# First group's queries and keys through the SP and ACT queues, by halves of the heads

## The chip, the cores and the metric

The kernel runs on one core of one Trainium2 chip. The metric is the device time of one execution in microseconds (us). TensorE is called PE here, VectorE DVE, ScalarE ACT, GpSimd POOL and SyncE SP; each runs its own instructions in program order and waits for the others by semaphores.

## The reference

Sliding-window attention with sink keys, then a feed-forward layer with a quick GELU (cut to what is computed):

```python
# q, k, v: 4 batches x 8 heads x 768 rows x 64, fp32; n_sink = 4, window = 128
scores = scale * np.matmul(q, k.transpose(0, 1, 3, 2))
rel = pos[:, None] - pos[None, :]
keep = (pos[None, :] < n_sink) | ((rel >= 0) & (rel < window))
scores = np.where(keep, scores, -1000000000.0)
a = np.exp(scores - np.max(scores, axis=-1, keepdims=True))
a = a / (np.sum(a, axis=-1, keepdims=True) + 1e-09)
attn_out = np.matmul(a, v)
x = attn_out.transpose(0, 2, 1, 3).reshape(3072, 512)
h = x @ w_in                                  # 512 x 2048
out = (h * (1.0 / (1.0 + np.exp(-1.702 * h)))) @ w_out    # 2048 x 512
```

## The kernel before

The 3072 tokens are worked through in twelve groups `g` of 256 rows (three to a batch `b`), each of two blocks `i` of 128 rows. A group goes through three stages, and successive groups overlap: attention, `hidden` (w_in and GELU), `out_part` (w_out). The order of the instructions on every engine is the order in which the program writes them; nothing rearranges them. For the first groups that order is written out by hand (L495 to L657), then a loop runs.

Attention of a group. `load_qk(g)` issues four loads on POOL (L124), for q and k of the two blocks, 128 rows by 512 columns (eight heads of 64) each; a load from POOL also casts fp32 to fp16. They go to the tile `qkn`. `transposed_qk` turns `qkn` into `qkT` with the head columns on the partitions: for the early groups PE transposes 128x128 tiles into a PSUM bank and DVE or ACT copies the bank out (L161 to L165). The heads are handled in pairs: `hp` is 0 to 3, two heads to each, so one `hp` is one 128-column tile.

The four sink keys of a batch are copied from `qkT` into `kd` (`sink_keys`, L168). `sinks(g)` (L185) makes the sink scores of all four `hp` by eight matmuls, then DVE scales and masks them into `sn` (L197) and takes their row minimum into `m2` (L203). `scores(g, hp)` makes the window scores of one `hp` (L231, L233) in a bank `nat`; there are two such banks, so the scores of hp 2 must wait until the weights of hp 0 have been read out of theirs. `maxima(g, hp)` is three DVE instructions: a predicated copy (L247), a row maximum (L250) and the bias (L260), which uses `m2`. `weights(g, hp)` is four exponentials on ACT (L271), by that bias. `weights_transposed` brings them to `AT`; for the first group by PE and a copy on DVE or ACT. `upper` and `lower` cut out the triangles, on POOL (L347) or DVE (L329). `sink_terms` (L302, tile `ts`) needs the bias of all four `hp`; `sink_weights` (L311) and `sink_transposed` (L316) follow. `values` (L360 to L372) multiplies by `vs` (the sinks' values spread over 16 column groups, filled by `sink_values`, L177, and a cast of `sinkrows`, L462) and by `vn`, the group's values; `normal` divides by the row sums, and `x_transposed` gives `xT`. Then `hidden(0, 0)` begins (L420).

At the start, before any of that: SP loads `ident` and `sinkrows`, then eight small pieces of v (`vsr`); ACT loads three constants and then its table of the exponential (`preload_act_table`, L453); DVE clears tiles; POOL issues `load_qk(0)`, then `load_w_in(0)`, `load_qk(1)`, `load_v(0)` and the other three quarters of w_in. The part of the written-out order that matters here (`ahead(0, 0)` is `sinks(0)`, `scores(0, 0)`, `maxima(0, 0)`; `ahead(0, 1)` the last two for hp 1):

```python
    transposed_qk(0, (0,))
    sink_values(0)
    transposed_qk(0, (1,))
    sink_keys(0, nc.vector.tensor_copy)
    ahead(0, 0)
    ahead(0, 1)
    weights(0, 0)
    weights(0, 1)
```

Of the kernel before, what the change touches and what calls it, by code (L numbers as in the profile page):

```python
# [10 lines left out]
FP32 = mybir.dt.float32  # L11
# [6 lines left out]
P = 128  # L18
D = 64
# [16 lines left out]
def _own() -> np.ndarray:  # L36

    return np.triu(np.ones((P, P))).astype(np.float16)


def _sink_off(n_sink: int) -> np.ndarray:


    q, j = np.arange(P)[:, None], np.arange(n_sink)[None, :]
    m = np.zeros((P, 2, 8, n_sink), np.float32)
    m[:, 0] = BIG
    m[:, 1] = np.where(q >= j, 0.0, BIG)[:, None, :]
    return m.reshape(P, 16 * n_sink)
# [10 lines left out]
def kernel(  # L59
# [34 lines left out]
    vs = [big.tile([P, 16, D + 1], FP16, name=f"vs{b}") for b in range(B)]  # L94
    vsr = big.tile([64, B, D], FP32, name="vsr")
    pace = big.tile([1, 1], FP32, name="pace")

    def constant(eng, name, array, dt):
        d = nc.inline_tensor(array, name="c" + name)
        t = const.tile(list(array.shape), dt, name=name)  # L100
        eng.dma_start(t, d.ap())
        return t
# [4 lines left out]
    def av_bank(name, shape, dt=FP32):  # L107
        return psp.tile(list(shape), dt, tag="av", bufs=2, name=name)
# [17 lines left out]
    def load_qk(g: int):  # L126
        for part in range(4):
            load_part(g, part)

    def load_v(g: int):  # L130
        for part in (4, 5):
            load_part(g, part)

    def load_w_in(i: int):
        w = DF // 4
        nc.gpsimd.dma_start(
            w_in16[:, :, bass.ts(i, w)],
            moe_w_in[:, bass.ts(i, w)].rearrange("(c p) f -> p c f", p=P),
        )

    def load_w_out(i: int):
# [2 lines left out]
            moe_w_out[bass.ts(i, 512), :].rearrange("(c p) f -> p c f", p=P),  # L144
        )

    def transposed_qk(g: int, parts=range(2)):

        n = G[g]["qkn"]
        if 0 in parts:  # L150
            G[g]["qkT2"] = work.tile([P, 4 * HP, P], FP16, tag="qkT", bufs=4, name=f"qkT{g}")
        T = G[g]["qkT2"]
        if g >= EARLY:
            nc.sync.dma_start_transpose(T, n.rearrange("p a c -> p (a c)"))
        else:
            for part in parts:
                for a in (2 * part, 2 * part + 1):
                    first = g == 0 or (g == 1 and part == 0)
                    tp = (mm_bank if first else av_bank)(f"tqk{g}_{a}", (P, HP, P), FP16)
                    for c in range(HP):  # L160
                        nc.tensor.transpose(tp[:, c], n[:, a, bass.ts(c, P)], ident)  # L161
                    if (g == 1 and part == 0) or (g != 1 and a % 2 == 1):
                        nc.scalar.copy(T[:, bass.ts(a, HP)], tp)
                    else:
                        nc.vector.tensor_copy(out=T[:, bass.ts(a, HP)], in_=tp)  # L165
        G[g]["qkT"] = T.rearrange("p (e i c) s -> p e i c s", e=2, i=2)

    def sink_keys(b: int, copy):  # L168
        kT = G[b * NT]["qkT"]
        for h in range(2):  # L170
            copy(
                out=kd[b][bass.ts(h, D), :, bass.ts(h, n_sink)],
                in_=kT[bass.ts(h, D), 1, 0, :, 0:n_sink],
            )

    def sink_values(b: int):
        nc.vector.tensor_tensor(  # L177
            out=vs[b][0:64, :, 0:D],
            in0=vsr[:, b].unsqueeze(1).broadcast_to((64, 16, D)),
            in1=sink_rows[0:64].unsqueeze(2).broadcast_to((64, 16, D)),  # L180
            op=ALU.mult,
        )


    def sinks(g: int):  # L185

        b, t = divmod(g, NT)
        qkT = G[g]["qkT"]
        sk = av_bank(f"sk{g}", (P, 2, HP, 2 * n_sink))
        for i in range(2):  # L190
            for hp in range(HP):
                nc.tensor.matmul(sk[:, i, hp], qkT[:, 0, i, hp], kd[b][:, hp], start=True, stop=True)
        sn = work.tile([P, 16, n_sink], FP32, tag="sn", name=f"sn{g}")
        flat = sn.rearrange("p a j -> p (a j)")
        skf = sk.rearrange("p i a j -> p (i a j)")
        if t == 0:
            nc.vector.scalar_tensor_tensor(  # L197
                out=flat, in0=skf, scalar=-scale, in1=sink_off, op0=ALU.mult, op1=ALU.add
            )
        else:  # L200
            nc.vector.tensor_scalar(out=flat, in0=skf, scalar1=-scale, scalar2=None, op0=ALU.mult)
        m2 = work.tile([P, 2, HP, 2], FP32, tag="m2", name=f"m2{g}")
        nc.vector.tensor_reduce(out=m2.rearrange("p i c h -> p (i c h)"), in_=sn, axis=AX.X, op=ALU.min)  # L203
        G[g].update(sn=sn, m2=m2, bias=work.tile([P, 2, HP, 2], FP32, tag="bias", name=f"bias{g}"))

    def scores(g: int, hp: int):

# [35 lines left out]
    def maxima(g: int, hp: int):  # L243
        m1 = work.tile([P, 2, 2], FP32, tag="m1", name=f"m1{g}_{hp}")
        if ("whole", hp) in G[g]:
            nat = G[g]["whole", hp]
            nc.vector.copy_predicated(  # L247
                out=nat[:, :, :, P:], mask=kinds(take_prev, g % NT), data=nat[:, :, :, 0:P]
            )
            nc.vector.tensor_reduce(  # L250
                out=m1.rearrange("p h i -> p (h i)"), in_=nat.rearrange("p h i c -> p (h i) c")[:, :, P:],
                axis=AX.X, op=ALU.max,
            )
        else:
            for h in range(2):
                nc.vector.copy_predicated(
                    out=G[g]["nat", hp][h], mask=kinds(take_prev, g % NT)[:, h], data=G[g]["before", hp][h]
                )
            nc.vector.tensor_reduce(out=m1, in_=G[g]["mine", hp], axis=AX.X, op=ALU.max)
        nc.vector.scalar_tensor_tensor(  # L260
            out=G[g]["bias"][:, :, hp], in0=m1.rearrange("p h i -> p i h"), scalar=-scale,
            in1=G[g]["m2"][:, :, hp], op0=ALU.mult, op1=ALU.min,
        )

    def weights(g: int, hp: int):

        nat, bias = G[g]["nat", hp], G[g]["bias"]
        A = work.tile([P, 4, P], FP16, tag="A", bufs=4, name=f"A{g}_{hp}")
        for h in range(2):
            for i in range(2):  # L270
                nc.scalar.activation(  # L271
                    out=A[:, 2 * h + i], in_=nat[h][:, i], func=AF.Exp, bias=bias[:, i, hp, h : h + 1],
                    scale=scale,
                )
        G[g]["A", hp] = A
# [46 lines left out]
    def lower(g: int, hp: int, pool=False):  # L322

        AT, i0 = G[g]["AT", hp], int(g % NT == 0)
        lo = work.tile([P, 2, 2, P], FP16, tag="lo", bufs=4, name=f"lo{g}_{hp}")
        if pool:
            selected(lo, AT, i0, 1)
        else:
            nc.vector.tensor_tensor(  # L329
                out=lo[:, :, i0:], in0=AT[:, :, i0:], op=ALU.mult,  # L330
                in1=own.unsqueeze(1).unsqueeze(1).broadcast_to((P, 2, 2 - i0, P)),
            )
        G[g]["lo", hp] = lo
# [112 lines left out]


    ident = constant(nc.sync, "ident", np.eye(P, dtype=np.float16), FP16)
    load_qk(0)
    take_prev = constant(nc.scalar, "prev", _take_prev(), U16)  # L450
    sink_off = constant(nc.scalar, "sinkoff", _sink_off(n_sink), FP32)
    own = constant(nc.scalar, "own", _own(), FP16)
    nc.scalar.preload_act_table(AF.Exp)  # L453
    sink_rows = constant(nc.sync, "sinkrows", _sink_rows(), FP32)
# [3 lines left out]
    masked_l = const.tile([P, P], FP16, name="maskedl")  # L458
    masked_r = const.tile([P, P], FP16, name="maskedr")
    sinkA = [const.tile([P, P], FP16, name=f"sinkA{i}") for i in range(2)]  # L460
    nc.vector.memset(vs[0], 0.0)
    nc.vector.tensor_copy(out=vs[0][:, :, D : D + 1], in_=sink_rows.unsqueeze(2))  # L462
    nc.vector.memset(masked_l, -1000.0)
    nc.vector.memset(masked_r, 15624.0)
    for t_ in (*kd, *sinkA):
        nc.vector.memset(t_, 0.0)
    for row in vn:
        for t_ in row:
            nc.vector.memset(t_[:, :, :, D : D + 1], 1.0)
    zero_reg = nc.gpsimd.to_reg(0.0)  # L470
    load_w_in(0)
    load_qk(1)
    load_v(0)
    for i in (1, 2, 3):
        load_w_in(i)

    def sink_columns(b: int):
        nc.vector.memset(vs[b], 0.0)
# [2 lines left out]
    def ahead(n: int, hp: int):  # L481

        if n < NG:
            if hp == 0:
                sinks(n)
            scores(n, hp)
            maxima(n, hp)
# [4 lines left out]
                out_part(g, i, p)  # L492


    transposed_qk(0, (0,))  # L495
    sink_values(0)
    transposed_qk(0, (1,))
    sink_keys(0, nc.vector.tensor_copy)
    ahead(0, 0)
    ahead(0, 1)  # L500
    weights(0, 0)
    weights(0, 1)
    scores(0, 2)
# [1 line left out]
    maxima(0, 2)  # L505
    upper(0, 0)
    lower(0, 0, pool=True)
    weights(0, 2)
    scores(0, 3)
    maxima(0, 3)  # L510
    sink_terms(0)
    weights_transposed(0, 1, by_act)
    upper(0, 1)
    lower(0, 1, pool=True)
    sink_weights(0)
    weights(0, 3)
    sink_transposed(0)
# [242 lines left out]
```

## Time and profile before

| what | value |
|---|---|
| median of three runs | 256.85 us (254.86 to 257.67) |
| the profiled execution | 253.48 us |
| its span, first to last instruction | 251.8 us |
| PE busy | 220.5 us, 88% of the span |
| DVE, ACT, POOL busy | 60%, 61%, 40% |
| granted PE clock | 0.99 of full speed |
| moved by DMA | 32.86 MB, mean 131 GB/s |

The page of the profile gives the busy time of each engine, the same in 40 slices of the span, the DMA queues, the chain of work that ended last with each step's releaser, and the costliest groups of instructions. The trace behind it answers finer questions: the chain within a window, the instructions of a window in order of time with what ended the idle time before each, and the busy time of each engine by window. In the lists "ACTq" and "SPq" are the engines' sequencers, which issue DMAs; the time of such a row is that of the issue, not of the transfer.

### The profile page before, as it was taken

Reading aid. Unit: us, or ns where it says so; the run is one execution under the profiler, and the core shown is the slowest. Engines: PE = TensorE matmul, PEld = TensorE weight load, DVE = VectorE, ACT = ScalarE, POOL = GpSimd, SP = SyncE. Lnnn points to the kernel's source line nnn. Section 1 sums busy time; section 2 is a strip of 40 time slices with the busy share of each in tenths; the row PEclk is TensorE's granted clock in tenths of the full one; section 3 lists DMA queues with packets and bytes.
Section 4 is the critical chain, followed back from the end, with each engine's and each line's share of the span. In section 5 each row is a group of like instructions: output and inputs, shape, how many; then the busy total and the mean of one; then the engine's idle time right before and its main releaser. Section 6 shows DMA issues by size and latency. Waiting matters only on the chain.

```text
span 251.8 us, 5731 instructions
## 1 busy us (share of the span) xinstructions
PE 220.5 (88%) x2180; PEld 151.2 (60%) x2180; DVE 151.5 (60%) x397; ACT 153.9 (61%) x349; POOL 101.6 (40%) x154
## 2 busy tenths in 40 slices
PE   0437979797785999999999999999999999799993
PEld 0326756674354848738758569478486595494851
DVE  4686777386589647657768288477583783830101
ACT  2176575748457577676766875776777767751430
POOL 8848547423662825816624445356020220310000
PEclk9999999999998899999999999999999999999999
DMA  8999999989699999999999989999965623603102
GB/s 77 157 176 198 188 194 123 160 107 98 116 144 175 153 131 169 165 119 246 115 158 160 144 169 144 133 172 140 163 131 98 108 63 64 146 3 83 42 3 85
DMA packets 133612, 32.86 MB, mean 131 GB/s; under 512 B 126288, under 2 KB 130512, under 8 KB 133584
## 3 DMA queue, kind: packets, MB, share of 16 engines
q0 software_dynamic: 79104, 13.64, 73.7%
q1 hardware_dynamic: 54048, 18.73, 42.2%
q8 instruction: 17, 0.28, 0.5%
q10 hardware_dynamic: 432, 0.13, 0.2%
q14 instruction: 11, 0.09, 0.1%
HBM read 27.50 MB, written 6.29 MB: 134 GB/s over the span
## 4 chain that ended last, share of the span: by engine, by line
PE 51%; DVE 17%; ACT 16%; DMA 10%; issue 4%; POOL 0%; ACTq 0%; DVEq 0%; POOLq 0%; SPq 0%
PE hT L420 27%; PE o L435 12%; ACT A L271 7%; DVE m L250 5%; DVE nat L247 5%; DMA AT<-A 5%; ACT L423 4%; DMA xT<-xn 3%; PE av L372 2%; ACT L271 2%; ACT gT L423 2%; DMA qkn<-in_q_dram 2%; PE av L360 2%; PE av L368 2%; PE tqk L161 1%
## 5 line engine op out<-in xcount | busy, mean ns | idle before, releaser
L420 PE MATMUL hT<-xT,w_in 128*128 128x256 f16 x768 | 95.6, 275 | 5.4 <-ACT gT L423 2.4
L435 PE MATMUL o<-w_out,gT 128*128 128x512 f16 x384 | 89.6, 379 | 0.0
L420 PEld LDWEIGHTS <-w_in 128*128 128x128 f16 x768 | 72.8, 99 | 18.6 <-issue 3.5
L423 ACT ACTIVATE gT<-hT 128x512 f16<-128x512 f32 x96 | 56.5, 597 | 44.4 <-PE hT L420 44.2
L347 POOL TENSOR_SCALAR_AFFINE_SELECT up<-AT 128x512 f16<-128x512 f16 (+1 forms) x48 | 28.0, 588 | 103.6 <-DMA AT<-A 76.6
L271 ACT ACTIVATE A<-nat,bias 128x128 f16<-128x128 f32 x192 | 53.4, 383 | 24.4 <-DVE bias L260 19.2
L435 PEld LDWEIGHTS <-gT 128*128 128x128 f16 x384 | 34.9, 98 | 37.8
L247 DVE COPY_PREDICATED nat<-prev,nat 128x512 f32<-128x512 uint16 x40 | 27.7, 692 | 24.3 <-PE nat L233 11.1
L250 DVE TENSOR_REDUCE m<-nat 128x4 f32<-128x512 f32 x40 | 27.6, 691 | 1.4
L329 DVE TENSOR_TENSOR lo<-AT,own 128x512 f16<-128x512 f16 (+1 forms) x44 | 19.1, 448 | 5.8 <-DMA AT<-A 5.6
L124 POOL DMA_DIRECT2D qkn<-in_k_dram x24 | 21.3, 896 | 2.8 <-DMA w_out<-in_moe_w_out_dram 2.8
L124 POOL DMA_DIRECT2D qkn<-in_q_dram x24 | 21.6, 905 | 1.3 <-POOLq L741 0.8
L124 POOL DMA_DIRECT2D vn<-in_v_dram x24 | 21.2, 891 | 1.0 <-issue 0.8
L390 DVE TENSOR_TENSOR xn<-av,rcp 128x256 f16<-128x256 f32 x48 | 20.4, 424 | 1.7
L443 DVE COPY osb<-o 128x512 f32<-128x512 f32 x10 | 6.9, 691 | 23.2 <-PE o L435 23.2
L368 PE MATMUL av<-vn,up 128*128 128x65 f16 x160 | 18.6, 195 | 1.1 <-POOL up L347 1.1
L372 PE MATMUL av<-vn,lo 128*128 128x65 f16 x160 | 18.3, 196 | 0.7 <-POOL lo L347 0.6
L360 PE MATMUL av<-vs,AsT 128*128 128x130 f16 x80 | 16.6, 224 | 0.4 <-DVE xn L390 0.3
L389 DVE RECIPROCAL rcp<-av 128x4 f32<-128x4 f32 x48 | 8.5, 178 | 13.8 <-PE av L372 13.5
L368 PEld LDWEIGHTS <-up 128*128 128x128 f16 x160 | 14.9, 100 | 2.4 <-POOL up L347 1.3
L233 PE MATMUL nat<-qkT 64*128 64x128 f16 x272 | 16.0, 224 | 0.0
L233 PEld LDWEIGHTS <-qkT 64*128 64x128 f16 x352 | 11.4, 97 | 7.1 <-issue 6.9
(59 smaller groups left out, 184.6 us busy)
## 6 DMA issues: line engine op xcount, KB each, us to landing
out_dram<-osb SPq DMA_DIRECT2D x24, 256.0 KB
qkn<-in_q_dram POOLq DMA_DIRECT2D x24, 128.0 KB, 5.2
qkn<-in_k_dram POOLq DMA_DIRECT2D x24, 128.0 KB, 4.8
vn<-in_v_dram POOLq DMA_DIRECT2D x24, 128.0 KB, 6.4
w_in<-in_moe_w_in_dram POOLq DMA_DIRECT2D x4, 512.0 KB, 9.8
w_out<-in_moe_w_out_dram POOLq DMA_DIRECT2D x4, 512.0 KB, 10.1
AT<-A SPq DMA_TRANSPOSE x40
qkT<-qkn SPq DMA_TRANSPOSE x9
```

The costliest lines, as they stand in the source:

```text
L124: nc.gpsimd.dma_start(dst, (q, k, v)[e][b, :, rows].rearrange("h s d -> s h d"))
L233: nc.tensor.matmul(to[h][:, i], qkT[r, 0, i, hp], keys[r], start=True, stop=True)
L247: nc.vector.copy_predicated(out=nat[:, :, :, P:], mask=kinds(take_prev, g % NT), data=nat[:, :, :, 0:P])
L250: nc.vector.tensor_reduce(out=m1.rearrange("p h i -> p (h i)"), in_=nat.rearrange("p h i c -> p (h i) c")[:, :, P:], axis=AX.X, op=ALU.max,)
L271: nc.scalar.activation(out=A[:, 2 * h + i], in_=nat[h][:, i], func=AF.Exp, bias=bias[:, i, hp, h : h + 1], scale=scale,)
L347: nc.gpsimd.affine_select(out=out, in_=in_, pattern=[[0, rows], [sign, P]], compare_op=ALU.is_gt if sign < 0 else ALU.is_ge, fill=zero_reg ...
L360: nc.tensor.matmul(av[:, i].rearrange("p h d -> p (h d)"), AsT, vs[b][:, c : c + 2].rearrange("p h d -> p (h d)"), start=True, stop=False,)
L368: nc.tensor.matmul(av[:, i, h], up[:, h, i], vn[b][J // 2][:, J % 2, head], start=False, stop=False)
L372: nc.tensor.matmul(av[:, i, h], own_w[:, h, i], vn[b][t][:, i, head], start=(I == 0), stop=(I == 0 or h == 1))
L420: nc.tensor.matmul(hT[:, f], w_in16[:, c, bass.ts(F, P)], xT[:, :, c], start=(c == 0), stop=(c == 3))
L423: nc.scalar.activation(out=G[g]["gT"][:, 2 * F2 : 2 * F2 + 2].rearrange("p f s -> p (f s)"), in_=hT.rearrange("p f i s -> p (f i s)"), fun ...
L435: nc.tensor.matmul(o, gT[:, F, bass.ts(i, P)], w_out16[:, F], start=(F == 0), stop=(F == NF - 1))
```

## The change

The first group's q and k no longer come through POOL. Four new fp32 tiles `first[e][u]` (e: q or k; u: first or second half of the heads) are loaded without a cast, q from SP and k from ACT, two loads each (one a block); the first halves are issued before `prev` and `sinkoff`, the second halves after them and before `own` and the table load. DVE rounds the q halves to fp16, ACT the k halves (`first_rounded`). `first_transposed(u)` transposes half of the heads of q and k into one PSUM bank and copies it out in two copies. `sink_keys` and `sinks` take a range of `hp`, so that sink scores, `sn` and `m2` of the first group are made for hp 0 and 1 first, then for hp 2 and 3; other groups call them as before.

Around it the order changes: the memsets of the ones columns of `vn` move from DVE to POOL; `load_v(0)` becomes POOL's first load; w_in 2 and 3 are issued later, behind the triangles of hp 0 and of hp 1; the memset of `vs[0]` moves behind the other memsets, and its cast and `sink_values(0)` move from the start to behind `maxima(0, 3)`, ahead of `sink_terms(0)`.

```diff
+    first = [[big.tile([P, 2, 4 * D], FP32, name=f"first{e}_{u}") for u in range(2)] for e in range(2)]
...
+    def load_first(eng, e: int, u: int):
+
+        for i in range(2):
+            eng.dma_start(
+                first[e][u][:, i].rearrange("s (h d) -> s h d", h=4),
+                (q, k)[e][0, 4 * u : 4 * u + 4, bass.ts(i, P)].rearrange("h s d -> s h d"),
+            )
+
+    def first_rounded(e: int, u: int, copy):
+        copy(G[0]["qkn"][:, 2 * e : 2 * e + 2, bass.ts(u, 4 * D)], first[e][u])
+
+    def first_transposed(u: int, copies):
+        n = G[0]["qkn"]
+        T = G[0]["qkT2"].rearrange("p (e i c) s -> p e i c s", e=2, i=2)
+        tp = mm_bank(f"tqk0_{u}", (P, 2, 2, 2, P), FP16)
+        for e in range(2):
+            for i in range(2):
+                for c in range(2):
+                    nc.tensor.transpose(tp[:, e, i, c], n[:, 2 * e + i, bass.ts(2 * u + c, P)], ident)
+        for e in range(2):
+            copies[e](T[:, e, :, 2 * u : 2 * u + 2], tp[:, e])
...
-    def sinks(g: int):
+    def sinks(g: int, pairs=slice(0, HP)):
...
-            for hp in range(HP):
+            for hp in range(pairs.start, pairs.stop):
                 nc.tensor.matmul(sk[:, i, hp], qkT[:, 0, i, hp], kd[b][:, hp], start=True, stop=True)
...
     ident = constant(nc.sync, "ident", np.eye(P, dtype=np.float16), FP16)
-    load_qk(0)
+    load_first(nc.sync, 0, 0)
+    load_first(nc.scalar, 1, 0)
     take_prev = constant(nc.scalar, "prev", _take_prev(), U16)
     sink_off = constant(nc.scalar, "sinkoff", _sink_off(n_sink), FP32)
+    load_first(nc.sync, 0, 1)
+    load_first(nc.scalar, 1, 1)
     own = constant(nc.scalar, "own", _own(), FP16)
     nc.scalar.preload_act_table(AF.Exp)
...
-    nc.vector.memset(vs[0], 0.0)
-    nc.vector.tensor_copy(out=vs[0][:, :, D : D + 1], in_=sink_rows.unsqueeze(2))
+    for row in vn:
+        for t_ in row:
+            nc.gpsimd.memset(t_[:, :, :, D : D + 1], 1.0)
+    zero_reg = nc.gpsimd.to_reg(0.0)
     nc.vector.memset(masked_l, -1000.0)
     nc.vector.memset(masked_r, 15624.0)
     for t_ in (*kd, *sinkA):
         nc.vector.memset(t_, 0.0)
-    for row in vn:
-        for t_ in row:
-            nc.vector.memset(t_[:, :, :, D : D + 1], 1.0)
-    zero_reg = nc.gpsimd.to_reg(0.0)
+    nc.vector.memset(vs[0], 0.0)
+    load_v(0)
     load_w_in(0)
     load_qk(1)
-    load_v(0)
-    for i in (1, 2, 3):
-        load_w_in(i)
+    load_w_in(1)
...
-    transposed_qk(0, (0,))
-    sink_values(0)
-    transposed_qk(0, (1,))
-    sink_keys(0, nc.vector.tensor_copy)
-    ahead(0, 0)
-    ahead(0, 1)
+    first_rounded(0, 0, by_dve)
+    first_rounded(1, 0, by_act)
+    first_transposed(0, (by_dve, by_act))
+    first_rounded(0, 1, by_dve)
+    first_rounded(1, 1, by_act)
+    scores(0, 0)
+    scores(0, 1)
+    sink_keys(0, nc.vector.tensor_copy, slice(0, 2))
+    sinks(0, slice(0, 2))
+    maxima(0, 0)
+    first_transposed(1, (by_act, by_act))
+    maxima(0, 1)
+    sink_keys(0, nc.vector.tensor_copy, slice(2, HP))
+    sinks(0, slice(2, HP))
     weights(0, 0)
     weights(0, 1)
     scores(0, 2)
...
     maxima(0, 2)
     upper(0, 0)
     lower(0, 0, pool=True)
+    load_w_in(2)
     weights(0, 2)
     scores(0, 3)
     maxima(0, 3)
+    nc.vector.tensor_copy(out=vs[0][:, :, D : D + 1], in_=sink_rows.unsqueeze(2))
+    sink_values(0)
     sink_terms(0)
     weights_transposed(0, 1, by_act)
     upper(0, 1)
     lower(0, 1, pool=True)
+    load_w_in(3)
     sink_weights(0)
```

More of the change, by code (lines that the diff above doesn't have):

```diff
@@ L166, in transposed_qk, with sink_keys @@
         G[g]["qkT"] = T.rearrange("p (e i c) s -> p e i c s", e=2, i=2)
-    def sink_keys(b: int, copy):
+    def sink_keys(b: int, copy, pairs=slice(0, HP)):
         kT = G[b * NT]["qkT"]
@@ L171, in sink_keys @@
             copy(
-                out=kd[b][bass.ts(h, D), :, bass.ts(h, n_sink)],
-                in_=kT[bass.ts(h, D), 1, 0, :, 0:n_sink],
+                out=kd[b][bass.ts(h, D), pairs, bass.ts(h, n_sink)],
+                in_=kT[bass.ts(h, D), 1, 0, pairs, 0:n_sink],
             )
@@ L182, in sink_values @@
         )
-    def sinks(g: int):
+    def sinks(g: int, pairs=slice(0, HP)):
         b, t = divmod(g, NT)
         qkT = G[g]["qkT"]
-        sk = av_bank(f"sk{g}", (P, 2, HP, 2 * n_sink))
+        if pairs.start == 0:
+            G[g].update(
+                sn=work.tile([P, 16, n_sink], FP32, tag="sn", name=f"sn{g}"),
+                m2=work.tile([P, 2, HP, 2], FP32, tag="m2", name=f"m2{g}"),
+                bias=work.tile([P, 2, HP, 2], FP32, tag="bias", name=f"bias{g}"),
+            )
+        sk = av_bank(f"sk{g}_{pairs.start}", (P, 2, HP, 2 * n_sink))
@@ L190, in sinks @@
         for i in range(2):
-            for hp in range(HP):
+            for hp in range(pairs.start, pairs.stop):
                 nc.tensor.matmul(sk[:, i, hp], qkT[:, 0, i, hp], kd[b][:, hp], start=True, stop=True)
-        sn = work.tile([P, 16, n_sink], FP32, tag="sn", name=f"sn{g}")
-        flat = sn.rearrange("p a j -> p (a j)")
-        skf = sk.rearrange("p i a j -> p (i a j)")
+        if pairs == slice(0, HP):
+            sn4, m2f = G[g]["sn"], G[g]["m2"].rearrange("p i c h -> p (i c h)")
+            sn = sn4.rearrange("p a j -> p (a j)")
+            skp, off = sk.rearrange("p i a j -> p (i a j)"), sink_off
+        else:
+            sn4 = G[g]["sn"].rearrange("p (i c h) j -> p i (c h) j", i=2, h=2)[
+                :, :, 2 * pairs.start : 2 * pairs.stop
+            ]
+            sn = G[g]["sn"].rearrange("p (i a) j -> p i (a j)", i=2)[
+                :, :, 2 * n_sink * pairs.start : 2 * n_sink * pairs.stop
+            ]
+            m2f = G[g]["m2"].rearrange("p i c h -> p i (c h)")[:, :, 2 * pairs.start : 2 * pairs.stop]
+            skp = sk.rearrange("p i a j -> p i (a j)")[:, :, 2 * n_sink * pairs.start : 2 * n_sink * pairs.stop]
+            off = sink_off.rearrange("p (i a) -> p i a", i=2)[
+                :, :, 2 * n_sink * pairs.start : 2 * n_sink * pairs.stop
+            ]
@@ L196, in sinks @@
         if t == 0:
             nc.vector.scalar_tensor_tensor(
-                out=flat, in0=skf, scalar=-scale, in1=sink_off, op0=ALU.mult, op1=ALU.add
+                out=sn, in0=skp, scalar=-scale, in1=off, op0=ALU.mult, op1=ALU.add
             )
         else:
-            nc.vector.tensor_scalar(out=flat, in0=skf, scalar1=-scale, scalar2=None, op0=ALU.mult)
-        m2 = work.tile([P, 2, HP, 2], FP32, tag="m2", name=f"m2{g}")
-        nc.vector.tensor_reduce(out=m2.rearrange("p i c h -> p (i c h)"), in_=sn, axis=AX.X, op=ALU.min)
@@ L204, in sinks @@
-        G[g].update(sn=sn, m2=m2, bias=work.tile([P, 2, HP, 2], FP32, tag="bias", name=f"bias{g}"))
+            nc.vector.tensor_scalar(out=sn, in0=skp, scalar1=-scale, scalar2=None, op0=ALU.mult)
+        nc.vector.tensor_reduce(out=m2f, in_=sn4, axis=AX.X, op=ALU.min)
     def scores(g: int, hp: int):
@@ L492, in o @@
                 out_part(g, i, p)
-    transposed_qk(0, (0,))
-    sink_values(0)
-    transposed_qk(0, (1,))
-    sink_keys(0, nc.vector.tensor_copy)
-    ahead(0, 0)
-    ahead(0, 1)
+    G[0]["qkn"] = work.tile([P, 4, DM], FP16, tag="qkn", bufs=3, name="qkn0")
+    G[0]["qkT2"] = work.tile([P, 4 * HP, P], FP16, tag="qkT", bufs=4, name="qkT0")
+    G[0]["qkT"] = G[0]["qkT2"].rearrange("p (e i c) s -> p e i c s", e=2, i=2)
+    first_rounded(0, 0, by_dve)
[12 more added lines that the diff above has]
+    sinks(0, slice(2, HP))
     weights(0, 0)
```

## The prediction

> **What bounds the kernel now.** The page's first two blocks come first: TensorE is busy 88% of the span, and its row of slices is thin only at the start and the very end. So I read the chain of waits for the first 30 us, then the timeline of the same stretch. The chain (start, length, what):
>
> ```profile
> 1.31 1.00 POOL qkn L124
> 2.32 4.97 DMA qkn<-in_q_dram
> 7.34 0.62 PE tqk L161 x4
> ...
> 8.62 0.60 PE tqk L161 x4
> 9.24 0.44 DVE qkT L165
> ...
> 10.32 0.36 PE sk L192 x8
> ...
> 11.26 0.71 DVE nat L247
> 11.99 0.70 DVE m L250
> ...
> 18.18 0.23 DVE ts L302
> ...
> 18.43 0.27 ACT sinkA L311
> ...
> 24.53 1.03 PE hT L420 x8
> ```
>
> Three parts: to 9.7 the chain waits for q and k; from 11.26 to 18.18 VectorE runs four maxima one behind the other; then the sink weights, the last transposes and values lead to the first hidden matmul at 24.53. From there TensorE is fed: in the table of windows it is busy 8.5 to 8.7 of every 10 us from 20 to 60, and no hT matmul of the first group waits for w_in. I therefore take it that the end moves by what 24.53 moves.
>
> The timeline shows what lies beside the chain:
>
> ```profile
> 1.69 0.45 ACTq L101 DMA_DIRECT2D own<-cown  x1
> 2.18 1.28 ACT L453 ACT_TABLE_LOAD   x1 [2.18 <-issue]
> 3.36 0.20 DVE L462 CAST vs<-sinkrows 128x16 f16<-128x16 f32 x1 [1.34 <-DMA sinkrows<-csinkrows]
> 6.43 1.22 DVE L177 TENSOR_TENSOR vs<-vsr,sinkrows 64x1024 f16<-64x1024 f32 x1 [0.20 <-DMA vsr<-in_v_dram]
> 9.70 0.57 DVE L171 COPY kd<-qkT 64x16 f16<-64x16 f16 x2
> 14.89 0.69 DVE L247 COPY_PREDICATED nat<-prev,nat 128x512 f32<-128x512 uint16 x1 [0.48 <-PE nat L233]
> ```
>
> The table load stands behind ACT's constants. The vs product, 1.22, runs in VectorE's idle time. Between the maxima VectorE idles only once to speak of (0.48).
>
> **The loads.** Four POOL loads (0.90 to 1.01 each to issue) leave the head; their data was in at 5.2, 7.3, 8.0 and 8.6 or a little later, by when TensorE could use it. In their place come eight loads of 128 KB (128 rows, four heads, 256 B pieces), four each on SP and ACT. No row of the trace issues such a load. Nearest are the constants, 0.35 to 0.46 (one piece a row), and the vsr loads, 0.67 to 0.93 (strided pieces). I take 0.5 each, since the load covers 128 rows as the constants do, and keep 0.35 and 0.93. Landing: sinkrows was issued at 1.23 and used at 3.36, so 2.1 us of latency; the DMA rows of the first 4 us reach 269 GB/s, so the first four loads (0.5 MB) need about 2 us more at 250. The first halves are in near 4.3, against 7.3 and 8.6.
>
> A rule speaks against this. The Trainium skill, "DMA: Bandwidth & Descriptors", section "Issuing engines are not separate DMA queues", says that DMAs from any engine share the same 16 DMA engines, and that several issuers save only issue time. By that alone the data would come little earlier, and the time would be that of the third rival below. I set a row above it: in the DMA view of the first 10 us, in slices of 0.25, the DMA engines stand at 0 until 1.75 and mostly at 40 to 50% until 3.5; what fills them then is POOL's loads of q and k, which the change takes away. In that stretch issue time is the limit.
>
> **ACT's queue is the new head.** Its loads stand before the table load, and rounding k stands behind that. From 0.81: two loads 1.0, prev 0.37, sinkoff 0.46, two loads 1.0, own 0.45, table 1.28 give 5.4. In the trace the later vsr loads wait for the constants' completion counts (hardware loads take turns on eight counts); ACT's third and fourth load are then about the ninth and eleventh and wait for the first ones' landing: 0.6 more, so 6.0. Rounding k costs 0.59 (ACT's 128x512 copy), so 6.65; four transposes of k 0.62, 7.3; ACT's copy to qkT 0.59, 7.95. q is done beside that (its DVE rounding, 0.42 to 0.69 by the copies of f16 and f32, ends near 5). Then TensorE: two hp of scores at 0.4, so the half sinks start at 8.75 (kd's copies, 0.5, lie beside), 0.25 for them, sn 0.23 and m2 0.22 with 0.15 between: the first copy-predicate at 9.65 instead of 11.26. Lead 1.6. With 0.35 a load it is 2.0; with 0.93 the queue alone is 1.7 longer, of which the 0.6 wait is absorbed: lead 0.5.
>
> **VectorE gives it back.** Before, 11.26 to 18.18 is 6.92: four maxima at a pitch of 1.54 (11.26 to 12.80), that is 6.16, and 0.76 of small waits (0.48 for the scores of hp 2, the rest at hp 3 and ts). After, the same row holds: two maxima 3.08; kd's second half, two copies, 0.55; the way to TensorE and back for the second half sinks 0.34; second sn and m2 0.50 (two half-width instructions cost nearly what the whole ones did: 0.23 and 0.22 for 64 elements are mostly fixed); two maxima 3.1; the cast of sink columns 0.2; the vs product 1.26; hand-over 0.1. Sum 9.1. The scores of hp 2 and 3 are then no longer waited for: the weights of hp 0 (ACT, from 11.3, 1.15) free their bank at 12.5, before the second half sinks. So ts starts at 9.65 + 9.1 = 18.75 instead of 18.18: **0.6 later**. Behind ts stand the sink weights on ACT, behind them the weights of hp 3 (1.13), the last transposes, values, xT and the first hidden matmul. All of them wait, so 24.53 becomes 25.1. The vs product is 1.26 of this: its cover, the wait for q and k, is what the change leaves.
>
> **Costed at nothing.** Twelve memsets go from DVE (0.07 each, idle time) to POOL ahead of its first load: POOL's memsets start 0.03 apart, its slowest small copy takes 0.20, so 0.4 to 2.4. v's two loads still start by 4 instead of 9.13, and need at most 10.5 to land; values begin at 19.86. w_in 2 and 3 are issued near 16 and 18 instead of 13.1 and 14.1; at the worst landing of 11.9 they are in by 28 and 30, for first use near 30.5 and 32.5. That is enough, and POOL's stream is four loads shorter, so I charge 0, at worst 0.5. SP's vsr loads move behind four loads and are in by 12, used at 17.5. POOL's selects move with the weights.
>
> One more rule speaks against the roundings: the Trainium skill, "SBUF — State Buffer", section "SBUF: two separate sides", says that an fp32 SBUF copy on VectorE can lock GpSimd out of writing load descriptors. The trace has only a related case, the vs product beside POOL's loads at 5.66 to 7.48, which kept their 0.91. By the rule v's or w_in's issue would slip by the two roundings, up to 1.4; they have several us to spare, so the sum is the same.
>
> **Rivals.**
> 1. *Faster, downstream.* POOL's stream of loads is four loads shorter and starts w_in and v sooner, so it drains 2 to 3 us earlier near 44. Then the key transposes of group 3 and the loads of group 4 end sooner, and the weight transposes at 61.3 and 64.0 (2.43 and 3.16 on the chain) meet less traffic. If half of that falls away, 2.8 is gained: 0.6 - 2.8 = -2.2, 254.6; a third gives -1.3. Against: those loads are paced by POOL's place in the chain, so they come along with it.
> 2. *Slower, ACT's head.* A 512-piece load costs more than any row here shows. Each 0.1 us per load puts 0.4 on ACT's queue ahead of the table load. It decides from 1.15 us a load on: four times 0.65 is 2.6, less the 0.6 wait, gives 2.0, plus 0.6 is 2.6. At 1.3 us: +3.2, 260.0.
> 3. *It does not do what it says.* Eight loads share the DMA engines with prev, sinkoff and v; the first halves land no earlier than before (7.3). Then k is rounded at 7.9, transposed at 8.55, in qkT at 9.2, 1.25 later than forecast: +1.85, 258.7.
>
> **How the numbers follow.** The profiled execution took 253.48 with a span of 251.8 (1.7 around it); the median of the runs is 256.85, 3.4 above it. The sum, 253.48 + 0.6 = 254.1, carried to the median gives 257.45. The forecast case (leads of 2.0 to 0.5, so +0.2 to +1.7: 257.0 to 258.6) gets 0.52, the rivals 0.18, 0.18 and 0.12. Runs of one kernel spread by 2.8, so a median of three can be 1 to 1.5 off, and 1% (2.6 us) is about the least that tells a change here. Low end: a third of the waits of rival 1 with such noise, 255; high end: rival 2 at 1.3 us, 260. Above 1% slower: most of rival 2 (0.13), some of rival 3 (0.04) and the noise of the forecast (0.04), 0.21. Above 1% faster: half of rival 1 (0.09) and 0.02. The rest, 0.68, is within 1%.
>
> **What would show it.** Right: ACT's table load ends near 6, the first copy-predicate stands near 9.7, ts behind the vs product near 18.8, the first hT matmul near 25.1. Rival 2: ACT's loads over 1.1 us each. Rival 3: VectorE's first rounding not before 6.5. Rival 1: hT late as forecast, but the AT transposes of the 61 to 67 us stage shorter. I am wrong if ts starts before 18, that is if VectorE's second half of kd, sn, m2 and the vs product hide somewhere.

## The result and the profile after

The change makes the kernel slower. Twenty runs each have a median of 254.32 us before and 257.89 after; the ratio is 1.0135 (95% interval 1.0113 to 1.0157), 3.4 us. The profiled execution of the changed kernel took 259.53 (span 257.8), the third longest of its twenty; so its rows are read for order and cause and the sizes come from the ratios, which count only executions within 1.5% of the fastest of their kernel (17 of 20 here, 5 of 10 in e5_hold_own, 5 of 6 in g1_hw_all, all or all but one in the other new kernels, one of 453.28 us in e4_pool_halves being left out).

The chain of waits of the changed kernel at the start (start, length, what):

```profile
1.21 3.44 DMA first<-in_q_dram
4.67 9.56 DMA first<-in_k_dram
...
14.32 0.63 ACT qkn L337
14.99 0.62 PE tqk L166 x4
15.63 1.07 ACT qkT L337 x2
16.70 1.05 ACT A L311 x4
...
21.78 1.09 DVE vs L200
22.87 0.35 DVE ts L342
...
29.26 1.03 PE hT L460 x8
```

One load holds the chain from 4.67 to 14.23: the last of ACT's, the second block of k's second half of the heads. The first hidden matmul starts at 29.26 instead of 24.53. The timeline of ACT shows how it hangs together ("ACTq" rows are the issues of loads):

```profile
0.81 1.00 ACTq L151 DMA_DIRECT2D first<-in_k_dram  x2
...
3.29 1.77 ACTq L151 DMA_DIRECT2D first<-in_k_dram  x2
6.33 0.35 ACTq L102 DMA_DIRECT2D own<-cown  x1
6.71 1.28 ACT L496 ACT_TABLE_LOAD   x1 [6.71 <-DMA first<-in_q_dram]
8.01 0.62 ACT L337 CAST qkn<-first 128x512 f16<-128x512 f32 x1
9.78 0.58 ACT L337 COPY qkT<-tqk 128x512 f16<-128x512 f16 x1 [1.16 <-DVE qkT L334]
14.32 0.62 ACT L337 CAST qkn<-first 128x512 f16<-128x512 f32 x1 [3.95 <-DMA first<-in_k_dram]
```

Two things are to be seen. The table load, and with it the first rounding of k, waits until 6.71, because the issue of `own` in front of it waited until 6.33 for the completion count of an earlier load of q. And the second rounding of k finds ACT idle for 3.95: its data is not there. By the completion counts in the trace the eight loads, issued at 0.81 to 4.67, landed at 3.3 and 5.4 (k) and 4.7 and 6.3 (q) for the first half, at 7.9 and 9.1 (q) and 10.5 and 14.2 (k) for the second. POOL's loads of v and w_in, issued from 1.62 on, run beside them: the DMA packets of POOL's queue begin at 4.2.

The order on ACT adds a smaller loss behind that. The bias of hp 0 is ready at 13.5, but ACT's program has the late rounding and the two copies ahead of the exponentials of hp 0, so these start at 16.70 and the bank that the scores of hp 2 need comes free only after the first four of them, at 17.8. The prediction had that bank free at 12.5; here VectorE waits another 0.69 for those scores, ahead of its third predicated copy at 18.51.

### The profile page after: what moved, and what is told of

Read it like the earlier page. It is cut to its first block, busy times and chain, and to the rows that moved or that the text cites. A ratio compares the mean times of both kernels' runs of the same rounds, so it can differ in the third digit from the quotient of the medians.

```text
span 257.8 us, 5742 instructions
## 1 busy us (share of the span) xinstructions
PE 220.8 (86%) x2180; PEld 150.8 (59%) x2180; DVE 151.9 (59%) x390; ACT 155.4 (60%) x352; POOL 99.7 (39%) x162
## 4 chain that ended last, share of the span: by engine, by line
PE 54%; DVE 14%; DMA 14%; ACT 14%; issue 3%; ACTq 0%; SPq 0%; POOL 0%; DVEq 0%; POOLq 0%
PE hT L460 29%; PE o L475 13%; DMA xT<-xn 6%; ACT A L311 5%; DVE m L290 4%; DVE nat L287 4%; DMA first<-in_k_dram 4%; ACT L463 3%; DMA AT<-A 2%; PE av L412 2%; ACT gT L463 2%; PE av L400 2%; PE av L408 2%; PE nat L273 1%; DMA first<-in_q_dram 1%
## 5 line engine op out<-in xcount | busy, mean ns | idle before, releaser
L387 POOL TENSOR_SCALAR_AFFINE_SELECT up<-AT 128x512 f16<-128x512 f16 (+1 forms) x48 | 29.0, 609 | 111.9 <-DMA AT<-A 85.2
L369 DVE TENSOR_TENSOR lo<-AT,own 128x512 f16<-128x512 f16 (+1 forms) x44 | 17.3, 407 | 6.0 <-DMA AT<-A 5.9
L125 POOL DMA_DIRECT2D qkn<-in_k_dram x22 | 19.5, 895 | 2.6 <-DMA w_out<-in_moe_w_out_dram 2.3
L125 POOL DMA_DIRECT2D qkn<-in_q_dram x22 | 19.6, 899 | 0.8 <-issue 0.7
L400 PE MATMUL av<-vs,AsT 128*128 128x130 f16 x80 | 16.5, 223 | 0.7 <-DVE xn L430 0.7
L429 DVE RECIPROCAL rcp<-av 128x4 f32<-128x4 f32 x48 | 8.5, 178 | 12.9 <-PE av L412 12.5
```

Of the source, the lines that this page charges most:

```text
L125: nc.gpsimd.dma_start(dst, (q, k, v)[e][b, :, rows].rearrange("h s d -> s h d"))
L387: nc.gpsimd.affine_select(out=out, in_=in_, pattern=[[0, rows], [sign, P]], compare_op=ALU.is_gt if sign < 0 else ALU.is_ge, fill=zero_reg ...
L400: nc.tensor.matmul(av[:, i].rearrange("p h d -> p (h d)"), AsT, vs[b][:, c : c + 2].rearrange("p h d -> p (h d)"), start=True, stop=False,)
```

## The experiments

Three theories were set against each other. A: the loads on SP and ACT share the DMA engines with POOL's long stream and come off badly. B: they are issued too late, behind waits for completion counts. C: the excess lies in VectorE's new order, the vs product above all.

**POOL held.** One small copy on POOL, which reads the last k load, is put ahead of its first load:

```diff
+    nc.gpsimd.tensor_copy(out=pace, in_=first[1][1][0:1, 1, 0:1])
     load_v(0)
```

> POOL waits with all its loads (v, w_in, group 1) until the second half of k has landed; nothing else changes. Theory A (the loads on SP and ACT share the DMA engines with POOL's stream and get too little of them): the second half of k, rounded at 14.3 us in the changed kernel, is rounded near 8 to 9, the first hT matmul falls from 29.3 to about 25.5, and the time falls by 2 to 3.5 us below the changed kernel (ratio to before 1.000 to 1.006). Theory B (the second half of k is late because ACT issues it late, at 3.3 and 4.7 us, behind the waits for completion counts): it still lands after 11 us and the ratio stays above 1.01. Theory C (the excess lies in VectorE's order, the vs product ahead of ts): no change in the ratio, 1.013.

Ratio 1.0062 (1.0034 to 1.0091): more than half of the loss is gone. POOL's packets now begin at 10.0. ACT's timeline in this kernel:

```profile
3.31 1.45 ACTq L151 DMA_DIRECT2D first<-in_k_dram  x2
5.70 0.34 ACTq L102 DMA_DIRECT2D own<-cown  x1
6.08 1.28 ACT L496 ACT_TABLE_LOAD   x1 [6.08 <-DMA first<-in_q_dram]
7.37 0.62 ACT L337 CAST qkn<-first 128x512 f16<-128x512 f32 x1
9.14 0.58 ACT L337 COPY qkT<-tqk 128x512 f16<-128x512 f16 x1 [1.16 <-DVE qkT L334]
9.63 0.62 ACT L337 CAST qkn<-first 128x512 f16<-128x512 f32 x1
```

ACT issues its second pair of loads at nearly the same times as before (3.31 and 4.36 against 3.29 and 4.67), yet the second rounding no longer waits for data: the two loads landed at 7.4 and 8.0 instead of 10.5 and 14.2. That is theory A; B would have left them late. The ratio lies just above A's 1.000 to 1.006, below B's 1.01. The first hidden matmul starts at 26.75, a little later than A expected, since the first predicated copy still comes at 11.28: `own` and the table load have hardly moved.

**All eight loads ahead of the constants.**

```diff
     load_first(nc.sync, 0, 0)
     load_first(nc.scalar, 1, 0)
+    load_first(nc.sync, 0, 1)
+    load_first(nc.scalar, 1, 1)
     take_prev = constant(nc.scalar, "prev", _take_prev(), U16)
     sink_off = constant(nc.scalar, "sinkoff", _sink_off(n_sink), FP32)
-    load_first(nc.sync, 0, 1)
-    load_first(nc.scalar, 1, 1)
```

> All eight loads of the first group are issued ahead of prev and sinkoff; nothing else changes. Theory A: the last k load is issued near 3 us instead of 4.7 but still meets POOL's stream from 4 us on, so it lands between 9 and 12 us instead of 14.2, and the ratio to before is 1.005 to 1.012. Theory B: all halves are in by 7.5 us, the first hT matmul near 25.5, ratio 1.000 to 1.005. Theory C: ratio 1.013.

Ratio 1.0114 (1.0054 to 1.0175) from four executions. It lies within A's range and above all of B's, but the interval also holds C's 1.013, so the rows have to decide. k's second half, now issued at 1.83 and 2.39, landed at 6.3 and 8.4; but the last load of q, which SP issued at 3.34 (it waits for a count), landed at 11.3, and now VectorE waits for that, ahead of kd:

```profile
11.31 0.43 DVE L334 CAST qkn<-first 128x512 f16<-128x512 f32 x1 [1.59 <-DMA first<-in_q_dram]
```

So an earlier issue does help the load that gets it, and in this execution the load issued last is caught by POOL's stream: B names a part of A's condition, not another cause.

**The vs product behind ts.** `sink_terms(0)` moves ahead of the cast and `sink_values(0)`.

> The cast and the vs product stand behind ts on VectorE instead of ahead of it; nothing else changes. Theory C (the excess lies there): ts comes 1.4 us earlier against the last maximum and the first hT matmul 0.7 to 1.4 us earlier (the vs product now stands ahead of the copy of the transposed sink weights); ratio to before 1.008 to 1.010. Theory A and B: they grant the same gain, since k's wait lies ahead of it and this behind; the second half of k still lands near 14, so the ratio stays above 1.007.

Ratio 1.0084 (1.0043 to 1.0125). ts follows the last bias at once (20.67), and the first hidden matmul starts at 27.38. Not all of that 1.9 is the vs product: in this execution k's second half landed at 13.2, a microsecond sooner. The ratio is one that all three theories allowed, and its interval overlaps the changed kernel's, so by time this run neither separates them nor fixes the share of the vs product; e7 below has that product alone.

**Halves loaded by POOL.** The loads go to `qkn` with a cast, eight on POOL ahead of all others; the roundings fall away, the rest stays.

```diff
+    for u in range(2):
+        for e in range(2):
+            load_first(nc.gpsimd, e, u)
...
-                first[e][u][:, i].rearrange("s (h d) -> s h d", h=4),
+                G[0]["qkn"][:, 2 * e + i, bass.ts(u, 4 * D)].rearrange("s (h d) -> s h d", h=4),
...
-    first_rounded(0, 0, by_dve)
-    first_rounded(1, 0, by_act)
...
```

> The first group's halves are loaded by POOL with a cast, eight loads ahead of v, and not rounded by DVE and ACT; order, half scores and vs product stay as in the changed kernel. This leaves only the reordering of the change. By the prediction's sum VectorE's part costs 2.2 us from the first predicated copy to ts; with loads in POOL's own order the first halves land near 6 to 7 and the second near 9 (before: 7.3 and 8.9), so the first predicated copy comes near 10.5, the first hT matmul near 25.5 to 26, ratio to before 1.003 to 1.007 under theory A. If the ratio stays at 1.013, the loads on SP and ACT are not the cause.

Ratio 1.0001 (0.9966 to 1.0037), better than expected: POOL's half loads issue in 0.76 to 0.89 and land at 4.3 to 6.7 and 7.2 to 9.4, the first predicated copy stands at 9.76 and the first hidden matmul at 25.16. So with the halves loaded by POOL the reordering costs next to nothing by time: its first hidden matmul comes 0.6 later than before (25.16 against 24.53), as the prediction's sum for VectorE had it, and the ratio does not show that.

**POOL held and `own` on SP.**

```diff
-    own = constant(nc.scalar, "own", _own(), FP16)
...
     sink_rows = constant(nc.sync, "sinkrows", _sink_rows(), FP32)
+    own = constant(nc.sync, "own", _own(), FP16)
```

> As e1_hold, and the constant own is loaded by SP instead of ACT; it is used at 20 us. In e1_hold own's issue on ACT waited until 5.70 us for an earlier load's completion count and the table load (6.08 to 7.36) stood behind it. If ACT's queue is the head of the chain once k is no longer starved, the table load moves to about 4.75, the rounding of k to 6.1 and the first predicated copy from 11.28 to about 10.0; first hT matmul 25.5 instead of 26.75, ratio to before 1.001 to 1.004. If the landing of q and k is the head, nothing moves and the ratio stays at 1.006.

Ratio 0.9996 (0.9949 to 1.0044). The interval is wide: ten executions lie between 252.15 and 256.99, with a median of 255.68 against 254.03 for the kernel before, so the time alone doesn't settle this step. The rows moved as expected: the table load to 4.57 (4.75 expected), the first predicated copy to 9.78 (10.0), the first hidden matmul to 25.36 (25.5). ACT, then VectorE, in this kernel:

```profile
4.57 1.28 ACT L495 ACT_TABLE_LOAD   x1 [4.57 <-DMA first<-in_q_dram]
5.86 0.62 ACT L337 CAST qkn<-first 128x512 f16<-128x512 f32 x1
```

```profile
9.78 0.69 DVE L287 COPY_PREDICATED nat<-prev,nat 128x512 f32<-128x512 uint16 x1
...
17.64 1.21 DVE L200 TENSOR_TENSOR vs<-vsr,sinkrows 64x1024 f16<-64x1024 f32 x1
18.77 0.42 DVE L342 TENSOR_TENSOR ts<-bias,sn 128x64 f32<-128x64 f32 x1
```

The constant that ACT loaded for use at 20 us held the head of the chain by 1.5 us (11.28 to 9.78).

**The vs product alone.** The kernel before, with only the cast and `sink_values(0)` moved to behind `maxima(0, 3)`.

> The kernel before, with only the cast and the vs product moved to where the change puts them (behind the last maximum, ahead of ts). By the prediction's sum 1.4 us: ts from 18.2 to 19.6, first hT matmul from 24.5 to 25.9, ratio 1.004 to 1.007. If VectorE had slack there, nothing moves: ratio 1.000.

Ratio 1.0047 (1.0008 to 1.0086). VectorE in this kernel:

```profile
10.72 0.69 DVE L247 COPY_PREDICATED nat<-prev,nat 128x512 f32<-128x512 uint16 x1 [0.29 <-PE nat L233]
...
17.59 1.21 DVE L177 TENSOR_TENSOR vs<-vsr,sinkrows 64x1024 f16<-64x1024 f32 x1
18.72 0.41 DVE L302 TENSOR_TENSOR ts<-bias,sn 128x64 f32<-128x64 f32 x1
```

From the first predicated copy to ts it is 8.0 instead of 6.92 (18.18 - 11.26): the move alone costs 1.1 on the path; ts itself takes 0.41 instead of 0.23.

**Better versions.** Three steps were built on the halves loaded by POOL: the vs product back in VectorE's idle time ahead of the first copy to qkT (f1), q's and k's transposes in PSUM banks of their own (f2), the second half of kd copied by ACT (f3). A fourth kernel (g1) takes the SP and ACT loads with POOL held, `own` on SP, the vs product behind ts, the two banks and kd on ACT.

```diff
-    sink_keys(0, nc.vector.tensor_copy, slice(2, HP))
+    sink_keys(0, lambda out, in_: nc.scalar.copy(out, in_), slice(2, HP))
...
-        tp = mm_bank(f"tqk0_{u}", (P, 2, 2, 2, P), FP16)
+        tp = [mm_bank(f"tqk0_{u}_{e}", (P, 2, 2, P), FP16) for e in range(2)]
```

> As e4_pool_halves (halves loaded by POOL), with the cast and the vs product back in VectorE's idle time ahead of the first copy to qkT. If the vs product is 1.4 us of VectorE's chain, ts moves from 18.5 to 17.2 and the first hT matmul from 25.2 to 23.8: 0.7 us below the kernel before, ratio 0.995 to 0.999. If it is not on the chain, the ratio stays at e4's 1.000.

> As f1_pool_vs_early, with the transposes of q and of k in PSUM banks of their own, so that ACT's copy of k need not wait for VectorE's copy of q (0.46 us in e4_pool_halves). First predicated copy 0.4 us earlier than in f1 (near 9.4), first hT matmul near 23.4, ratio 0.993 to 0.997. If the second pair of banks is then waited for (there are two), the second half comes later and f1's time stays.

> As f2_pool_vs_banks, with the second half of kd copied by ACT (idle there) instead of VectorE. In f1 and f2 the 1.45 us between the second and third maximum are two kd copies (0.5), the way to TensorE and back, sn and m2. If this handover is what separates them, the third predicated copy moves from 14.23 to 13.2 to 13.4 (bound by the bank that the weights of hp 0 free near 12.6), ts from 17.4 to 16.5, the first hT matmul from 24.0 to 23.1; ratio to before 0.990 to 0.995. If the bank is the bound, the third copy stays above 14 and the ratio at 0.997.

> The changed kernel's loads on SP and ACT with every cost found so far taken off: POOL held until k is in, own on SP, cast and vs product behind ts, q's and k's transposes in banks of their own, second kd on ACT. e5_hold_own had the first predicated copy at 9.78 and ts at 18.77. Expected: first copy near 9.4, ts near 16.5, first hT matmul 23.3 to 24 (the vs product now delays the copy of the sink weights), ratio 0.991 to 0.997. If the loads on SP and ACT are worth anything over POOL's halves, it beats f3_pool_kd_act; by the first predicated copies (9.78 against 9.73) it does not.

| kernel | first predicated copy | ts | first hT | ratio to before (95%) |
|---|---|---|---|---|
| before | 11.26 | 18.18 | 24.53 | 1 |
| changed | 11.92 | 22.79 | 29.26 | 1.0135 (1.0113 to 1.0157) |
| e1_hold | 11.28 | 19.90 | 26.75 | 1.0062 (1.0034 to 1.0091) |
| e5_hold_own | 9.78 | 18.77 | 25.36 | 0.9996 (0.9949 to 1.0044) |
| e4_pool_halves | 9.76 | 18.51 | 25.16 | 1.0001 (0.9966 to 1.0037) |
| f1_pool_vs_early | 9.73 | 17.42 | 23.99 | 1.0008 (0.9973 to 1.0044) |
| f2_pool_vs_banks | 9.69 | 17.42 | 24.09 | 0.9972 (0.9937 to 1.0008) |
| f3_pool_kd_act | 9.71 | 17.20 | 23.86 | 0.9942 (0.9910 to 0.9975) |
| g1_hw_all | 9.87 | 16.71 | 23.96 | 0.9892 (0.9830 to 0.9954) |

f1 has its ts and first matmul where expected, but not its ratio. f2's interval holds no change (1), and its banks gained nothing at the first predicated copy: ACT's copy of k came 0.31 earlier than in f1 (7.28 against 7.59), and VectorE's first two kd copies then took 0.31 longer (1.12 against 0.81). f3 is the first that is clear of no change: a median of 252.70 against 254.42, at its expected ratio though not by the way expected. Its third predicated copy came at 13.28, as hoped, but ts only at 17.20 and the first hidden matmul at 23.86, where 16.5 and 23.1 were expected. VectorE in f3:

```profile
13.28 0.70 DVE L287 COPY_PREDICATED nat<-prev,nat 128x512 f32<-128x512 uint16 x1
14.01 0.69 DVE L290 TENSOR_REDUCE m<-nat 128x4 f32<-128x512 f32 x1
14.73 0.90 DVE L300 SCALAR_TENSOR_TENSOR bias<-m,m 128x4 f32<-128x4 f32 x1
15.56 0.68 DVE L287 COPY_PREDICATED nat<-prev,nat 128x512 f32<-128x512 uint16 x1
```

POOL in f3 at that time:

```profile
14.76 0.50 POOL L387 TENSOR_SCALAR_AFFINE_SELECT up<-AT 128x256 f16<-128x256 f16 x1
15.12 0.49 POOL L387 TENSOR_SCALAR_AFFINE_SELECT lo<-AT 128x256 f16<-128x256 f16 x1
```

The bias of hp 2, 0.16 in f1 and f2, ends when POOL's two selects end. g1 rests on six runs (median 253.05); its ratio is a little better than the 0.991 to 0.997 expected, while its first copy (9.87 for 9.4) and ts (16.71 for 16.5) come a little later. Its interval overlaps f3's, so which of the two is faster stays open, and so does whether loads on SP and ACT are worth anything over POOL's halves.

## Why the prediction went as it did

It forecast 0.6 us slower; the kernel became 3.4 us slower. That 257.4 lies near the measured 257.89 is luck: the median it started from, three runs of the kernel before, was 2.5 above that of twenty. Of the four signs it named for being right, none came in the changed kernel: the table load ended at 8.0, not near 6, the first predicated copy stood at 11.92 (9.7), ts at 22.79 (18.8), the first hidden matmul at 29.26 (25.1).

- **The price of an issue** (0.5, between 0.35 and 0.93) was right: ACT's rows are 0.39 to 0.53, SP's 0.50 to 0.58. Rival 2, over 1.15 a load, is out.
- **"The first halves are in near 4.3"** was 2 too early: 6.3 and 5.4, and with POOL held still 5.7 and 4.7. The two us for 0.5 MB left out that prev's packets and the second halves share the queues: with POOL held, those of SP and ACT had moved 0.88 MB by 5.7.
- **"In that stretch issue time is the limit"** is the step that failed. It set the Trainium skill's rule ("DMA: Bandwidth & Descriptors", section "Issuing engines are not separate DMA queues": DMAs of all issuers run on the same 16 engines and interleave) aside by the slices up to 3.5 us, and gave the second halves no landing time at all, though they are issued after 2.3 us; so their landing, the term that decided, was put at nothing. The change brings POOL's v and w_in forward into that time. Here the rule held: with nearly the same issue times (4.67 and 4.36) the last k load took 9.6 us beside POOL's stream and 3.6 without (e1), and the ratio fell from 1.0135 to 1.0062. Rival 3 had this mechanism, but on the first halves, and priced it at 1.85; its sign, a first rounding on VectorE not before 6.5, was nearly met (6.41).
- **ACT's queue as the new head** was right in kind. The table load was put at an end near 6; it ended at 8.0, because `own` waited for a count (until 6.33; 5.70 with POOL held). That wait was reckoned for the k loads only. (The lead of 2.0 at 0.35 a load was not worked out: four loads at 0.15 less would give 2.2, unless the wait grows.)
- **VectorE's 9.1** from the first predicated copy to ts was right: 8.99 in e5, where the data comes in time, and its times there are almost those of the forecast: 9.78 for 9.65, ts 18.77 for 18.75, first matmul 25.36 for 25.1. The vs product, put at 1.26 and 0.2 for its cast, costs 1.1 in all (e7).
- **The end moves with the first hidden matmul**: it moved by 4.73 in the profiled execution, the span by 6.0. The rest came at later transposes of that one execution, and no experiment was made on it. By the ratios the time moved by less than the matmul: by 1.6 us for 2.22 in e1, 2.9 for 3.58 in e2, 2.1 for 2.85 in e3 and 3.4 for 4.73 here, but by nothing for 0.54 earlier in f1. So this premise holds only roughly, and why is open. Rival 1, a gain downstream, was not seen: its two AT transposes took 2.43 and 3.22, against 2.43 and 3.16.

By the ratios: 0.7% is the starved k (1.0135 to 1.0062), and the next step, to 0.9996, would be 0.7% for the wait of `own`, which its rows support and its time, with that interval, does not settle. What is then left of the vs product and the half-wise sinks about balances what the early data gains.

## What to carry to other kernels

Give every load that a change moves a landing time of its own, the last one above all, by what else is in the DMA engines then; loads on another queue can come late, as here, if a long stream is let loose beside them, and here one small copy that held the stream back cost less than it gained. On an engine that computes, a constant's load can wait for a completion count and hold all behind it; give such constants to a queue that does nothing else. And what fills an engine's wait has to be placed anew when the wait goes.

## What the runs showed of the hardware

VectorE and POOL ran slower beside each other more than the prediction reckoned with. In the changed kernel POOL's select, usually 0.40, took 1.28 beside the vs product:

```profile
21.86 1.28 POOL L387 TENSOR_SCALAR_AFFINE_SELECT up<-AT 128x256 f16<-128x256 f16 x1 [0.72 <-ACT AT L337]
23.09 0.40 POOL L387 TENSOR_SCALAR_AFFINE_SELECT lo<-AT 128x256 f16<-128x256 f16 x1
```

The Trainium skill ("SBUF — State Buffer", section "SBUF: two separate sides") says that of a GpSimd instruction and certain VectorE instructions whichever starts first holds a shared port pair for its whole length. The select took 1.28 in all six kernels with the vs product ahead of ts, and 0.40 in f1, f2 and f3, where that product runs earlier. The prediction took from that page only that VectorE could hold up POOL's descriptors. Rows of the other direction stand here too. The bias in f3 took 0.90 instead of 0.16 and ended with the selects; in g1 the vs product took 2.00 beside selects and an issue instead of 1.21. The first two kd copies took 0.78 to 1.12 in e4, f1, f2 and f3, beside POOL's memsets and issues of v, and 0.33 to 0.57 in the kernels with loads on SP and ACT. VectorE's first rounding of q took 0.75 beside POOL's issues in the changed kernel, but 0.43 beside the same issues in e2 and e3. These are rows side by side; no experiment set one engine's work apart from the other's, so the cause is not shown.

One more row is not explained. The first eight hidden matmuls took 1.03 in the kernels before and changed, e3, e4, e5, e7 and f1, but nearly twice as long in e1, e2, f2, f3 and g1, at a granted clock of 1.00 in all; in e1:

```profile
26.75 1.86 PE hT L460 x8
```

No experiment tells why, and the table's column of first hidden matmuls does not hold these 0.8.
